# Feed-forward weight loads move from SyncE's DMA queue to GpSimd's in a fused attention and feed-forward block

## The chip, the cores and the metric

The kernel runs on one core of a Trainium2 chip. TensorE (PE) multiplies matrices, VectorE (DVE) and ScalarE (ACT) work element by element, GpSimd (POOL) is a third engine of that kind, and SyncE (SP) issues transfers. The metric is device time in microseconds of one execution; the kernel before took 827.6 us in the median of three runs (826.67, 827.6, 828.36).

## What is computed

One block of a diffusion transformer with adaptive layer norm, 2048 tokens of width 512, 32 heads of 16, and a gated feed-forward part of width 1792:

```
mod = silu(c) @ w_mod                       # six rows: sa, ca, ga, sb, cb, gb
h = layernorm(x) * (1 + ca) + sa
q, k, v = split_heads(h @ wqkv)             # 32 heads of 16
o = softmax(q @ k.T / 4) @ v
x = x + ga * (merge_heads(o) @ wo)
h = layernorm(x) * (1 + cb) + sb
x = x + gb * ((gelu(h @ w_gate) * (h @ w_up)) @ w_down)
```

All inputs and the output are bf16.

## The kernel before

The program is recorded by a planner and then written out. Every operation goes through `rec` (line 190), which finds the semaphores that the operation has to wait for, books it on an engine's list, and hands it to `model` (line 268). `model` keeps the planned free time of each engine and of the DMA engines; the planner places work by these times. The lists are then emitted engine by engine in the order of recording, so each engine, SyncE and GpSimd among them, runs its own list strictly in order. A wait stands ahead of the instruction that needs it and holds up everything behind it on that engine.

The queries are cut into seven sets (`SETS`: 512, 512, 256, 256, 256, 128 and 128 rows). For each set eight groups of four heads are walked, and for each group the keys in blocks. TensorE writes scores into six PSUM banks, three at a time (`qk`). ScalarE takes two or three of the three banks through its exponential into the ring `E`; where it takes two, VectorE takes the third, and makes the exponential from bit operations: one pass out of PSUM per bank (`bits`), and per four banks three passes over 2048 elements in SBUF, `mant`, `square` and `expo` in `power_task`. The products with the values add up in the bank `ps_pv`.

At the end of a group, `unit_end` (line 1554) sends the four softmax sums of each row through memory to have them reciprocated in a better layout: `scr_den<-osb`, `den<-scr_den`, a reciprocal on VectorE, `scr_rec<-rden` and four `rb<-scr_rec`. These are all DMAs on SyncE.

Between the scores, as "side" work, TensorE does the projections and, once a set is finished, its output projection and feed-forward part (`side_ffn`, line 940). For the first four sets (`flow`) the weights are streamed. Gate and up weights come in seven pieces each, of 128 x 4 x 256 elements (256 KB), into a ring of four slots, the columns 0 to 4095 of `mreg`. Four pieces are loaded at the start, and each consumed piece lets the piece four places later be loaded (`load(ci + 4)`, `load(nch + ci + 4)`). The down weights come in seven pieces of 128 x 2 x 512: three at the start into `dreg` (`load_down`), four later into the ring's slots. For the last three sets the whole set of weights is loaded once and kept: `weight_parts` (line 863) makes ten early pieces (`qT` and `xs` as their places), which the main loop issues while the third and fourth sets are worked on, and eleven late ones, issued once the fourth set is done.

All these loads are issued by SyncE, in the same list as the denominators' transfers and the output's. Three lines are enough to see the queue, the ring and the two resident lists:

```
self.dma("sp", ring[i % 4], v[:, :, 2 * P * ci:2 * P * ci + 2 * P], "st%d" % (i % 4))
self.dma("sp", self.wdst[i], v[:, 2 * i:2 * i + 2, :], "sd%d" % i)
return g[:6] + d[:4], u + g[6:] + d[4:]
```

GpSimd only sets some constants at the beginning.

Two more places are touched. `near_end` (line 905) sums the denominators of the last two sets with a matmul on TensorE (`self32`) in place of the way through memory. `fillers` (line 1352) yields matmuls without a use of their result, which keep TensorE busy; one of them writes into the bank `ps_mi`, when no side work has that bank open or when the side work at hand uses the sixth score bank in its place (`fifth`).

Of the kernel before, what the change touches and what calls it, by code (L numbers as in the profile page):

```python
# [14 lines left out]
P = 128  # L15
# [83 lines left out]
class _Recorder:  # L99
# [90 lines left out]
    def rec(self, eng, fn, reads=(), writes=(), dma=None, cost=0.0):  # L190

        if self.dry:
            return None
        stream = eng if dma is None else "d_" + dma
        seq = self.count.get(stream, 0) + 1
        needs = {}

        def need(s, n, raw):
            if s == stream and n == seq:
                return  # L200
            if s == eng == "pe" and dma is None:
                return
            if needs.get(s, 0) < n:
                needs[s] = n

        if dma is not None and seq > 1:
            needs[stream] = seq - 1
        acc = []
        for w, aps in ((False, reads), (True, writes)):
            for ap in aps:  # L210
                r = self._boxes(ap)
                if r is not None:
                    acc.append((w,) + r)
        for w, name, kind, bxs in acc:
            h = self.hist.get(name)
            if not h:
                continue
            for key, ent in h.items():
                for b in bxs:
                    if key[0] < b[1] and b[0] < key[1] and key[2] < b[3] and b[2] < key[3]:  # L220
                        lw, rd = ent
                        if lw is not None:
                            need(lw[0], lw[1], not w)
                        if w:
                            for s, n in rd.items():
                                need(s, n, False)
                        elif kind == "ps":
                            for s, n in rd.items():
                                if s != eng:
                                    need(s, n, False)  # L230
                        break
        at = 0.0
        for s, n in needs.items():
            at = max(at, self.bystream[s][n - 1].t1 + (30 if s == eng else 60))
        if self.probing is not None:
            self.probing = max(self.probing, at)
            self.asked = cost
            return None
        self.count[stream] = seq
        op = _Op(eng, stream, seq, fn)  # L240
        self.bystream.setdefault(stream, []).append(op)
        ck = self.clock[eng]
        for s, n in sorted(needs.items(), key=lambda x: -x[1]):
            if ck.get(s, 0) >= n:
                continue
            prod = self.bystream[s][n - 1]
            prod.inc = True
            op.waits[s] = n
            ck[s] = n
            for k, v in prod.clock.items():  # L250
                if ck.get(k, 0) < v:
                    ck[k] = v
        op.clock = dict(ck)
        for w, name, kind, bxs in acc:
            h = self.hist.setdefault(name, {})
            for b in bxs:
                if w:
                    for key in [k for k in h if b[0] <= k[0] and k[1] <= b[1] and b[2] <= k[2] and k[3] <= b[3]]:
                        del h[key]
                    h[b] = [(stream, seq), {}]  # L260
                else:
                    h.setdefault(b, [None, {}])[1][stream] = seq
        self.ops.append(op)
        self.model(op, max(at, self.free[eng]), cost)
        return op


    def model(self, op, t, cost):
        eng = op.eng
        if op.stream not in COMPUTE:  # L270
            size, run = cost
            self.free[eng] = t + 450
            self.dma_free = max(t + 900, self.dma_free) + size / (320 if run >= 1024 else 245 if run >= 512 else 200)
            op.t1 = self.dma_free + (1000 if run > 64 else 1500)
        elif eng == "pe":
            cols, rows, tp = cost
            mode = 0 if tp is None else (1 if rows == 32 else 2)
            t = max(t, self.pe_issue)
            if mode != self.pe_mode:
                t = max(t, self.pe_end + 105)  # L280
            q = range(16)
            if mode == 1:
                q = range(tp[0] // 8, tp[0] // 8 + 4)
            elif mode == 2:
                q = range(tp[1] // 32, 16, 4)
            t = max(t, max(self.tile_free[i] for i in q))
            end = t + max(cols, 64) / 2.4
            for i in q:
                self.tile_free[i] = end
            self.pe_mode, self.pe_issue, self.pe_end = mode, t + (4 if mode else 27), max(self.pe_end, end)  # L290
            self.free[eng] = t
            self.log.append((t, cols if mode == 0 else cols / 4))
            op.t1 = end + 158
        else:
            self.free[eng] = t + cost
            op.t1 = t + cost + (107 if eng == "act" else 92)
# [151 lines left out]
class _Kernel(_Recorder):  # L448
# [12 lines left out]
    def alloc(self):  # L461
# [32 lines left out]
        self.bufs += [(mreg[:, 4096 + 2048 * i:6144 + 2048 * i], "modB") for i in range(4)]  # L494
        self.bufs.append((wreg[:, 4096:6144], ("q", 3, 3)))
        self.held = set()
        self.two = self.fifth = False
        self.flowing = self.closing = False
        self.wo = sb("wo", [P, 8, D], BF16)
        self.E = sb("E", [P, NSL, 512], BF16)  # L500
# [362 lines left out]
    def weight_parts(self):  # L863

        def part(dst, src, sem):
            return lambda: self.dma("sp", dst, src, sem)
        gv = self.B_w_gate.rearrange("(a p) n -> p a n", p=P)
        uv = self.B_w_up.rearrange("(a p) n -> p a n", p=P)
        dv = self.B_w_down.rearrange("(f p) n -> p f n", p=P)
        g = [part(self.wg[i], gv[:, :, 256 * i:256 * i + 256], "wg%d" % i) for i in range(7)]  # L870
        d = [part(self.wd[i], dv[:, 2 * i:2 * i + 2, :], "wd%d" % i) for i in range(7)]
        u = [part(self.wu[i], uv[:, :, 256 * i:256 * i + 256], "wu%d" % i) for i in range(7)]
        return g[:6] + d[:4], u + g[6:] + d[4:]
# [31 lines left out]
    def near_end(self, k, qd, den):  # L905

        q0, W = SETS[k]
        yield from self.until(("osb", k, qd))
        _, lo, hi = self.osb_span(((k,), qd, q0, W))
        osb, rb = self.osb[:, lo:hi], self.rb[:, lo:hi]  # L910
        yield 4 * W, lambda: self.mm(den, self.self32[:, :], osb)

        def fin():
            self.tt("dve", self.onorm[:, qd, OCOL[k]:OCOL[k] + W], osb, rb, ALU.mult)
        if not self.dry:
            self.task([lambda: self.recip(rb, den)], ("rec", k, qd))
        yield from self.until(("rec", k, qd))
        if not self.dry:
            self.task([fin], ("onorm", k, qd))
        yield END  # L920
# [19 lines left out]
    def side_ffn(self, gi, begin=False):  # L940
# [13 lines left out]
        ring = self.wst[0] + self.wst[1]  # L954
        nch = len(chunks)

        def load(i):
            if flow and i < 2 * nch:
                v = (self.B_w_gate, self.B_w_up)[i // nch].rearrange("(a p) n -> p a n", p=P)
                ci = i % nch  # L960
                self.dma("sp", ring[i % 4], v[:, :, 2 * P * ci:2 * P * ci + 2 * P], "st%d" % (i % 4))
            elif flow:
                load_down(i - 2 * nch + 3)

        def load_down(i):
            if flow:
                v = self.B_w_down.rearrange("(f p) n -> p f n", p=P)
                self.dma("sp", self.wdst[i], v[:, 2 * i:2 * i + 2, :], "sd%d" % i)

        yield from self.until(("ln2", gi))  # L970
        self.flowing = self.flowing or not self.dry
# [200 lines left out]
    def stream(self):  # L1172
# [105 lines left out]
        def acc_of(u):  # L1278
            return self.scp[:, SC - 1, :] if u is units[1] else self.pv[:, :]
# [70 lines left out]
                    cg += 1  # L1350

        def fillers():
            if not self.open or self.fifth:
                yield lambda: self.mm(self.mi[:, :], *filler)
            w = self.next_side()
            if self.open and w is not None:
                self.first = None
                self.probe(w[4][1])
                if self.first is not None and self.first[0].shape[-1] >= P:
                    out, start = self.first  # L1360
                    x = filler[1][:, 0:int(out.shape[-1])]
                    yield lambda: self.mm(out, self.ident[:, :] if start else self.nil[:, :], x, start, start)
            u = next((u for u in units if group[u] == cg and u in begun and left[u]), None)
            if u is not None:
                yield lambda: self.pv_nil(acc_of(u)[:, 0:u[3]], filler[1])

        early, late = self.weight_parts()
        while cg <= group[units[-1]]:
# [7 lines left out]
            t = max(self.pe_now(), virt)  # L1376
# [364 lines left out]
```

## Time and profile before

| | |
|---|---|
| median of three runs | 827.6 us |
| the profiled execution | 826.18 us, span 824.5 us |
| granted TensorE clock | 1.00 |
| ACT busy | 794.4 us |
| DVE busy | 750.9 us |
| PE busy (matmuls) | 750.5 us |
| POOL busy | 4.6 us |
| moved by DMA | 43.73 MB in 76361 packets |
| DMA queue q1 | 76232 packets, 41.82 MB |

The span runs from the first to the last instruction of the profiled execution; the device time of the same execution is 1.7 us longer. Busy time is the sum of an engine's instructions, without waits and without the issuing of DMAs. In a row of instructions, `SPq` and `POOLq` are the sequencers that issue DMAs, `out<-in` are the program's tiles, and "us to landing" is the time from the issue of a DMA until its semaphore has its full count. A line number is often that of a helper (L337 is the matmul in `mm`, L355 the activation, L405 the DMA). TensorE writes 128x512 matmuls as four that use 32 columns of the array each, so one matmul of the source is four in the trace.

### The profile page before, as it was taken

The numbers are of one execution on the slowest core, as the hardware profiler recorded it, in microseconds if no ns is written. First come the engines' busy times: TensorE is split into PE (matmuls) and PEld (weight loads), VectorE is DVE, ScalarE is ACT, GpSimd is POOL, SyncE is SP. The second block draws the span as 40 slices with busy tenths as digits, with TensorE's granted clock in tenths as the row PEclk, the third lists the DMA queues.
The fourth block names the chain that finished last, engine by engine and source line by source line (L and its number), as shares of the span: only waits on it lengthen the run. The fifth ranks groups of instructions, "written<-read, shape, count | busy, mean of one in ns | idle before, by whom it ended". The sixth has DMA issues, their size and how long they took to land.

```text
span 824.5 us, 29810 instructions
## 1 busy us (share of the span) xinstructions
PE 750.5 (91%) x13502; PEld 293.0 (36%) x13502; DVE 750.9 (91%) x1342; ACT 794.4 (96%) x742; POOL 4.6 (1%) x13
## 2 busy tenths in 40 slices
PE   7999998888898998899998989999989989999998
PEld 3333332322222222222333333333443344345556
DVE  7857999999999999999999999999999999889964
ACT  5999999999999999999999999999999999999982
POOL 2000000000000000000000000000000000000000
PEclk9999999999999999999999999999999999999999
DMA  8100000000003211110013212210653243320000
GB/s 286 48 21 18 10 10 8 11 9 10 10 3 97 60 47 35 46 33 20 12 21 98 58 47 58 55 28 12 174 148 109 67 131 97 101 70 11 22 7 14
DMA packets 76361, 43.73 MB, mean 53 GB/s; under 512 B 20557, under 2 KB 74634, under 8 KB 76234
## 3 DMA queue, kind: packets, MB, share of 16 engines
q1 hardware_dynamic: 76232, 41.82, 18.3%
q8 instruction: 106, 1.74, 0.9%
q14 instruction: 21, 0.17, 0.1%
q10 hardware_dynamic: 2, 0.00, 0.0%
HBM read 39.18 MB, written 2.61 MB: 51 GB/s over the span
## 4 chain that ended last, share of the span: by engine, by line
ACT 88%; PE 6%; DVE 3%; DMA 2%; issue 0%; SPq 0%; DVEq 0%
ACT E L355 84%; PE ps_sc L337 3%; ACT hreg L355 3%; PE ps_mi L337 2%; ACT L355 2%; PE ps_pv L337 1%; DMA rb<-scr_rec 1%; DMA scr_rec<-rden 1%; DVE mreg L367 1%; DMA xs<-in_A_x_dram 0%; SPq L405 0%; DVE hreg L376 0%; DVE wreg L367 0%; DVE onorm L359 0%; DVE wreg L359 0%
## 5 line engine op out<-in xcount | busy, mean ns | idle before, releaser
L355 ACT ACTIVATE E<-ps_sc 128x1024 bf16<-128x1024 f32 (+2 forms) x704 | 749.9, 1298 | 14.5 <-PE ps_sc L337 14.2
L337 PE MATMUL ps_sc<-qT,kme 32*128 32x256 bf16 (+2 forms) x1600 | 193.1, 304 | 25.7 <-ACT E L355 21.8
L337 PE MATMUL ps_sc<-qT,kmo 32*128 32x256 bf16 (+2 forms) x1664 | 193.5, 298 | 21.3 <-ACT E L355 18.9
L367 DVE TENSOR_SCALAR mreg<-ps_sc 128x512 uint16<-128x512 f32 x272 | 182.2, 683 | 12.6 <-PE ps_sc L337 10.1
L337 PE MATMUL ps_pv<-E,vaug 128*17 128x256 bf16 (+2 forms) x2540 | 148.9, 300 | 0.9 <-DVE osb L376 0.7
L337 PE MATMUL ps_mi<-wreg,mreg 128*32 128x256 bf16 (+1 forms) x1920 | 110.2, 326 | 8.0 <-ACT hreg L355 2.4
L337 PEld LDWEIGHTS ps_sc<-qT,kme 32*128 32x128 bf16 x1600 | 53.4, 92 | 146.2 <-ACT E L355 124.7
L337 PEld LDWEIGHTS ps_sc<-qT,kmo 32*128 32x128 bf16 x1664 | 54.9, 92 | 132.6 <-ACT E L355 116.4
L367 DVE TENSOR_SCALAR dreg<-ps_sc 128x512 uint16<-128x512 f32 x136 | 91.3, 685 | 7.9 <-PE ps_sc L337 5.9
L337 PEld LDWEIGHTS ps_pv<-E,vaug 128*17 128x17 bf16 x2540 | 51.5, 89 | 53.3 <-issue 39.5
L367 DVE TENSOR_SCALAR mreg<-mreg 128x2048 uint16<-128x2048 uint16 x104 | 70.0, 681 | 0.1
L337 PEld LDWEIGHTS ps_mi<-wreg,mreg 128*32 128x32 bf16 x1920 | 42.4, 95 | 51.0 <-issue 19.6
L337 PE MATMUL ps_pv<-mreg,vaug 128*17 128x256 bf16 (+2 forms) x844 | 49.5, 298 | 3.1 <-DVE mreg L359 2.0
L359 DVE TENSOR_TENSOR mreg<-mreg 128x2048 bf16<-128x2048 bf16 x36 | 43.5, 1207 | 0.1
L337 PE MATMUL ps_mi<-hreg,wreg 128*32 128x512 bf16 x480 | 40.3, 385 | 0.4 <-DVE vaug L376 0.3
L359 DVE TENSOR_TENSOR dreg<-mreg,dreg 128x2048 bf16<-128x2048 bf16 x32 | 38.8, 1216 | 0.1
L359 DVE TENSOR_TENSOR hreg<-ps_mi,hreg 128x512 bf16<-128x512 f32 x48 | 32.8, 684 | 2.9 <-PE ps_mi L337 2.3
L359 DVE TENSOR_TENSOR mreg<-dreg,mreg 128x2048 bf16<-128x2048 bf16 x28 | 34.0, 1213 | 0.0
L337 PE MATMUL ps_mi<-wo,onorm 128*32 128x512 bf16 x416 | 32.1, 383 | 0.4 <-DVE qT L367 0.2
L376 DVE CAST hreg<-ps_mi 128x512 bf16<-128x512 f32 x46 | 31.4, 683 | 1.1 <-PE ps_mi L337 0.8
L337 PE MATMUL ps_mi<-xs,ident 128*32 128x512 bf16 (+1 forms) x376 | 30.7, 380 | 0.8 <-DVE hreg L359 0.8
L337 PE MATMUL ps_mi<-mreg,hreg 128*32 128x512 bf16 x384 | 31.1, 385 | 0.0
(161 smaller groups left out, 673.7 us busy)
## 6 DMA issues: line engine op xcount, KB each, us to landing
mreg<-in_B_w_up_dram SPq DMA_DIRECT2D x32, 256.0 KB, 3.0
mreg<-in_B_w_gate_dram SPq DMA_DIRECT2D x28, 256.0 KB, 3.5
mreg<-in_B_w_down_dram SPq DMA_DIRECT2D x16, 256.0 KB, 2.8
dreg<-in_B_w_down_dram SPq DMA_DIRECT2D x12, 256.0 KB, 4.6
mreg<-in_w_mod_dram SPq DMA_DIRECT2D x1, 2048.0 KB, 12.1
rb<-scr_rec SPq DMA_DIRECT2D x64, 32.0 KB, 1.8
out_dram<-xs SPq DMA_DIRECT2D x16, 128.0 KB, 1.7
rb<-scr_rec SPq DMA_DIRECT2D x116, 16.0 KB, 2.1
```

Of the source, the lines that this page charges most:

```text
L337: return self.rec("pe", lambda e: e.matmul(out, lhsT, rhs, start=start, stop=stop, tile_position=tp), [lhsT, rhs, *after], [out], cost=(n, ...
L355: return self.rec("act", lambda e: e.activation(out, in_, func, scale=scale, **kw), rd, wr, cost=self.cost("act", out, [in_], "act") + load)
L359: return self.rec(eng, lambda e: e.tensor_tensor(out, a, b, op), [a, b], [out], cost=self.cost(eng, out, [a, b], "tt"))
L367: return self.rec(eng, lambda e: e.tensor_scalar(out, a, s1, s2, **kw), rd, [out], cost=self.cost(eng, out, [a], "ts") + (60 if len(rd) > ...
L376: return self.rec(eng, lambda e: e.tensor_copy(out, in_), [in_], [out], cost=self.cost(eng, out, [in_], "ts"))
```

## The change

All loads of `w_gate`, `w_up` and `w_down`, streamed and resident, are issued by GpSimd. The planner goes on charging them to SyncE's planned time (`self.free["sp"]`), so that it places the rest as it did. A flag `sums` holds back the filler into `ps_mi` while a denominator sum lies there. The instructions on TensorE, VectorE and ScalarE, their order and their waits are the same in both programs; SyncE's list is shorter by 105 DMAs, GpSimd's is longer by as many. The loads keep their order among themselves.

```diff
@@ rec
-        self.model(op, max(at, self.free[eng]), cost)
+        self.model(op, max(at, self.free[eng if dma is None else "sp"]), cost)
@@ model
-            self.free[eng] = t + 450
+            self.free["sp"] = t + 450
@@ alloc
-        self.two = self.fifth = False
+        self.two = self.fifth = self.sums = False
@@ weight_parts
         def part(dst, src, sem):
-            return lambda: self.dma("sp", dst, src, sem)
+            return lambda: self.dma("pool", dst, src, sem)
@@ near_end
+        self.sums = True
         yield 4 * W, lambda: self.mm(den, self.self32[:, :], osb)
...
         yield from self.until(("rec", k, qd))
+        self.sums = False
@@ side_ffn
-                self.dma("sp", ring[i % 4], v[:, :, 2 * P * ci:2 * P * ci + 2 * P], "st%d" % (i % 4))
+                self.dma("pool", ring[i % 4], v[:, :, 2 * P * ci:2 * P * ci + 2 * P], "st%d" % (i % 4))
...
-                self.dma("sp", self.wdst[i], v[:, 2 * i:2 * i + 2, :], "sd%d" % i)
+                self.dma("pool", self.wdst[i], v[:, 2 * i:2 * i + 2, :], "sd%d" % i)
@@ fillers
-            if not self.open or self.fifth:
+            if not self.open or self.fifth and not self.sums:
```

GpSimd's list runs in order too. A load there waits for the matmuls that last read its place, and for nothing that stood between the loads in SyncE's list. The semaphores are unchanged.

## The prediction

> **What bounds the kernel now.** I read the busy totals first, then the chain that ended last, then the stretches in which feed-forward weights are loaded.
>
> ```profile
> span 824.5 us, 29810 instructions
> PE 750.5 (91%) x13502; PEld 293.0 (36%) x13502; DVE 750.9 (91%) x1342; ACT 794.4 (96%) x742; POOL 4.6 (1%) x13
> ACT 88%; PE 6%; DVE 3%; DMA 2%; issue 0%; SPq 0%; DVEq 0%
> 249.00:793.00 544.00, 500.49 (x9598) 197.75 (x9590) 513.61 (x885) 542.35 (x497) 0.00 (x0) 1.00 0.23 63
> 249.00:375.00 126.00, 113.72 (x1402) 31.86 (x1394) 122.43 (x194) 125.95 (x115) 0.00 (x0) 1.00 0.19 52
> 443.00:529.00 86.00, 78.63 (x1469) 29.08 (x1464) 81.00 (x139) 84.94 (x74) 0.00 (x0) 1.00 0.27 72
> 576.00:635.00 59.00, 53.24 (x1240) 26.14 (x1240) 55.19 (x94) 58.54 (x55) 0.00 (x0) 1.00 0.52 146
> 653.00:704.00 51.00, 46.20 (x1082) 22.18 (x1076) 49.43 (x88) 50.95 (x49) 0.00 (x0) 1.00 0.43 117
> ```
>
> The windows list, after length, the busy time of PE, weight loads, DVE, ACT and POOL. ScalarE's exponentials set the end. The first weights go out at 249.49 us (row below) and the last exponential ends near 793; there ScalarE is busy 542.35 of 544.00 us. So in the whole stretch that the change can touch, 1.65 us of ScalarE idle time is to be had, and no more. VectorE stands close behind: in the four loading windows its idle time is 3.57, 5.00, 3.81 and 1.57 us, 13.95 together.
>
> These are the places where ScalarE's feeding did break, from the chain in order of time:
>
> ```profile
> 474.01 0.07 SPq L405
> ...
> 475.81 3.35 DMA rb<-scr_rec
> ...
> 582.02 5.53 DMA scr_rec<-rden
> SPq L405 <- PE ps_mi L337: 56.8, 27, 5.9
> SPq L405 <- PE ps_sc L337: 46.8, 23, 7.1
> ```
>
> SyncE's queue is in order. It stands 103.6 us in total waiting for matmuls to release a weight buffer, and a softmax denominator's four small transfers queue behind such a wait: at 474 the chain passes through SyncE and then 3.35 us of a reciprocal's way back, at 582 through 5.53 us of its way out. That is what the change can mend.
>
> **The change, part by part.**
>
> *Two edits that only steer the planner* (SyncE's planned free time is charged for the loads as before; a filler is held back while a denominator sum lies in the shared bank): the two programs have the same instructions with the same waits on TensorE, VectorE and ScalarE. Cost nothing, with nothing to hide.
>
> *105 loads leave SyncE for GpSimd* (7 gate, 7 up and 7 down pieces for each of four streamed stages and for the resident set). Gain: SyncE's waits for TensorE go, so the denominators come earlier. ScalarE's idle time above bounds it at 1.65 us; below, at nothing, since VectorE may not be ready earlier either. The chain legs at 474 and 582 are part of it, not all: I take 0.7.
>
> *Earlier starts.* GpSimd's queue holds nothing else, so a stage's first seven loads go when the stage before has read its last down piece:
>
> ```profile
> 249.49 2.08 SPq L405 DMA_DIRECT2D mreg<-in_B_w_gate_dram  x4
> 410.32 0.40 PE L337 MATMUL ps_mi<-mreg,hreg 128*32 128x512 bf16 x4
> 443.50 2.09 SPq L405 DMA_DIRECT2D mreg<-in_B_w_gate_dram  x4
> 449.66 0.83 PE L337 MATMUL ps_mi<-wreg,mreg 128*32 128x512 bf16 x12
> 576.60 3.17 SPq L405 DMA_DIRECT2D mreg<-in_B_w_gate_dram  x4
> 580.91 0.84 PE L337 MATMUL ps_mi<-wreg,mreg 128*32 128x256 bf16 x24
> 582.45 2.59 SPq L405 DMA_DIRECT2D mreg<-in_B_w_gate_dram  x2
> 590.94 0.62 PE L337 MATMUL ps_mi<-wreg,mreg 128*32 128x256 bf16 x16 [0.35 <-DVE hreg L376]
> 619.12 0.42 SPq L405 DMA_DIRECT2D mreg<-in_B_w_down_dram  x1
> 624.77 0.61 PE L337 MATMUL ps_mi<-mreg,hreg 128*32 128x512 bf16 x8
> ```
>
> About 411 instead of 443.5 in the second stage. The shortest leads of a first piece, 449.66 - 443.50 = 6.2 and 580.91 - 576.60 = 4.3 us, grow, the first by some 33 us. Gain: none, since those matmuls didn't wait.
>
> *Loads in the middle of a stage* go as before, when the matmuls of four pieces back release their slot. The fifth piece of the third stage is issued at 582.45 and used at 590.94, 8.5 us later; the last down piece goes at 619.12 and is used at 624.77, 5.65 us later. The landing times of that window:
>
> ```profile
> mreg<-in_B_w_gate_dram SPq DMA_DIRECT2D x7, 256.0 KB, 4.2
> mreg<-in_B_w_down_dram SPq DMA_DIRECT2D x4, 256.0 KB, 3.0
> ```
>
> So 4.3 us (8.5 - 4.2) and 2.65 us (5.65 - 3.0) may be added before a matmul waits. If that cover goes, TensorE stands, the next scores are late, and ScalarE idles one for one.
>
> *What a load costs on GpSimd.* No row of before shows it, as GpSimd is done after 59 us. A gate or up piece is 128 x 4 runs of 512 bytes, 512 reads and 512 writes to be listed; a down piece is half as many of 1024 bytes. The nearest rows:
>
> ```profile
> 0.80 0.20 POOL L383 MEMSET nil<- 128x128 bf16 x1 [0.29 <-POOLq L1726]
> 2.17 2.26 POOL L383 MEMSET vaug<- 128x512 bf16 x1
> 4.03 1.25 POOL L383 MEMSET rb<- 128x1024 f32 x1
> 58.76 0.31 POOL L386 TENSOR_SCALAR_AFFINE_SELECT self<-self 128x128 f32<-128x128 f32 x1 [53.47 <-DVE self L383]
> L405 SPq DMA_DIRECT2D mreg<-in_B_w_up_dram x7: 368/378/505, 590.8 to 608.9; - x7
> ```
>
> Lower end: as quick as SyncE, 0.37 us. Upper end: 1,024 entries at the rate of the slow memset (2.26 us for 512), 4.5 us. I take the memset of 1,024 elements as nearest, one element an entry: 1.25 us for gate and up, and by the line through both quick memsets (0.20 + 384 x 1.05/896) 0.65 us for down. At that price the third stage's queue is 20 x 1.25 + 11 x 0.65 = 32 us of work in 59, and 1.25 us stays inside the 4.3 and 2.65 us of cover: no late matmul. At 4.5 us it would be some 115 us of work in 59.
>
> *What it costs VectorE.* VectorE is the next engine to become late. Two kinds of its passes stand out:
>
> ```profile
> L367 DVE TENSOR_SCALAR mreg<-ps_sc 128x512 uint16<-128x512 f32 x272 | 182.2, 683 | 12.6 <-PE ps_sc L337 10.1
> L367 DVE TENSOR_SCALAR mreg<-mreg 128x2048 uint16<-128x2048 uint16 x104 | 70.0, 681 | 0.1
> L367 DVE TENSOR_SCALAR dreg<-dreg 128x2048 uint16<-128x2048 uint16 x40 | 27.2, 679 | 0.0
> L367 DVE TENSOR_SCALAR dreg<-mreg 128x2048 uint16<-128x2048 uint16 x32 | 21.6, 683 | 0.0
> L367 DVE TENSOR_SCALAR mreg<-dreg 128x2048 uint16<-128x2048 uint16 x28 | 18.9, 679 | 0.0
> PEld ps_sc L337 <- DVE mreg L367: 3.6, 8, 0.9
> 714.27 2.13 SPq L405 DMA_DIRECT2D mreg<-in_B_w_up_dram  x4
> 704.00:793.00 89.00, 83.97 (x2132) 43.08 (x2124) 76.85 (x141) 88.95 (x86) 0.00 (x0) 1.00 0.18 47
> ```
>
> From SBUF to SBUF it does 2,048 elements in 0.68 us, from PSUM 512 in the same time. The wide passes (204, 0.25 per us of the span) use a path four times as wide; if GpSimd needs part of that path while it writes its lists, such a pass waits. A pass that wants to start while a load of length T is being written waits T/2 on average, so a load costs 0.25 x T x T/2: 0.195 us at 1.25, 0.053 at 0.65. Stages one, two and four: 14 x 0.195 + 7 x 0.053 = 3.1 us each; the third, with ten resident pieces among its own, 20 x 0.195 + 11 x 0.053 = 4.5. Lower end nothing (no shared path), upper end as T grows, by its square. The cover is VectorE's idle time of the window, of which I let two thirds help, because a delay has to meet idle time before a matmul needs the bank (the wait row: score matmuls already wait for VectorE's passes). What is left: 3.1 - 2.4 = 0.7; 3.1 - 3.3, nothing; 4.5 - 2.5 = 2.0; 3.1 - 1.05 = 2.05: 4.7 us. The last eleven loads, at 714, meet a stretch in which VectorE has 12 us to spare: nothing.
>
> The Trainium skill, page "SBUF — State Buffer", section "Who interferes with whom", says that VectorE and GpSimd share one pair of SBUF ports as an exclusive lock, taken by VectorE's two-port passes, and that a DMA issued from GpSimd needs it to write descriptors. The same page gives about 620 ns for such a DMA alone; as an estimate from that figure, 94 loads at 0.25 x 0.62 x 0.62/2 make 4.5 us, inside the cover, and the sum would be no change. No run here shows either yet.
>
> *Sum.* 826.2 (the profiled execution; span 824.5) + 4.7 - 0.7 = 830.2. The median of the runs shown, 827.6, is 1.4 above the profiled execution; I forecast 831.6 for a median.
>
> **The rivals.**
>
> *No change* (chance 0.27, 827.6 within 1.7): a load takes GpSimd well under 1 us, or the wide passes share nothing with it. For it: at T = 0.65 for all, 94 x 0.053 = 5 us fall inside VectorE's 13.95. Against: VectorE's idle time is 2 to 6% and in pieces.
>
> *Faster* (0.07): the freed SyncE queue is all that matters, and the denominators' way through memory no longer stands behind loads. Place: the chain legs at 474 and 582. Price: all 1.65 us of ScalarE's idle time, 825.9; it decides once VectorE loses less than some 1 us in all. Against: it has to recover every gap, and 31.5 us after 793 don't contain a load.
>
> The Trainium skill, page "DMA: Bandwidth & Descriptors", section "Issuing engines are not separate DMA queues", holds that another issuer saves only the sequencer's issue time. By that there is no gain either; the trace's bound agrees.
>
> *GpSimd too slow for the ring* (0.16): at T of 2 us or more the third stage's queue nears 40 + 11 us of 59 while the passes lose 62 x 0.5 + 32 x 0.125 = 35 us, 26 beyond the cover: 853; with 4.5 us per piece TensorE waits for weights too, 115 - 59 = 56 us in the third stage alone, 880 and over. Against: the nearest row is 1.25.
>
> *My forecast*, some microseconds lost through VectorE: 0.50, between 829.3 and 848 (at T = 1.8: 62 x 0.405 + 32 x 0.10 = 28.3, less 9.3 of cover, + 19).
>
> **How the numbers follow.** 0.2%, 1.7 us, is about what a measurement of this kernel tells from no change. Faster 0.07, same 0.27, slower 0.50 + 0.16 = 0.66. The likeliest gives 831.6. The range goes from 826.0 (the bound on the gain) to 848 (the forecast's end at T = 1.8); it leaves out half of the faster case and nearly all of the third rival, some 0.18. The forecast's own range is 829.3 to 848.
>
> **What would show it.** Right: wide passes of more than 0.68 us mean or gaps ahead of them, mostly between 249 and 704; more ScalarE idle time than 1.65 us there, released by score matmuls that waited for VectorE; the second stage's loads at about 411; SyncE's waits for TensorE gone. Wrong: passes unchanged with ScalarE idle as before (no change); matmuls on weights that wait for a DMA (the ring), and landing times of 6 us and more; or ScalarE's idle time below 0.5 us (faster). If VectorE's rows are unchanged and the time is longer all the same, the mechanism is wrong whatever the total.

## The result and the profile after

| | before | after |
|---|---|---|
| median | 827.6 us (826.67 to 830.12, 5 runs) | 837.07 us (835.56 to 838.9, 5 runs) |
| ratio | 1 | 1.0115, 95% interval 1.0099 to 1.0131 |
| span of the profiled execution | 824.5 us | 835.3 us |

The change costs 9.5 us between the medians, and the two profiled spans lie 10.8 us apart. From the page after: busy totals, GpSimd's DMA queue (packets, MB, share) and the shares of the chain that ended last.

```profile
PE 755.4 (90%) x13502; PEld 293.7 (35%) x13502; DVE 752.7 (90%) x1342; ACT 796.2 (95%) x742; POOL 84.4 (10%) x118
q0 software_dynamic: 8400, 27.53, 11.4%
ACT 72%; PE 13%; DVE 7%; DMA 7%; SPq 1%; issue 1%; DVEq 0%
```

The busy times of VectorE and ScalarE hardly moved (+1.8 us each), so the time went into waits. In the chain, ScalarE gave up 16 points; PE, DMA and VectorE took them. The windows after say where (columns as in the prediction: start and end, length, busy PE, weight loads, DVE, ACT, POOL, then the granted clock, the DMA share and GB/s; 576 to 635 and 704 to 793 are left out, the sum has them):

```profile
249.00:375.00 126.00, 114.02 (x1402) 31.73 (x1398) 122.66 (x194) 125.95 (x115) 10.34 (x14) 1.00 0.15 37
375.00:443.00 68.00, 60.33 (x971) 19.75 (x968) 61.67 (x100) 63.06 (x60) 5.44 (x7) 0.95 0.15 42
443.00:529.00 86.00, 78.68 (x1483) 29.38 (x1482) 82.55 (x146) 85.95 (x75) 10.35 (x14) 1.00 0.19 48
529.00:576.00 47.00, 44.25 (x860) 16.72 (x859) 43.33 (x80) 45.76 (x42) 5.16 (x7) 1.00 0.23 65
635.00:653.00 18.00, 15.51 (x288) 6.04 (x280) 14.84 (x28) 15.44 (x14) 5.15 (x7) 0.91 0.43 117
653.00:704.00 51.00, 45.95 (x1042) 21.38 (x1040) 47.52 (x88) 49.42 (x45) 9.68 (x12) 0.97 0.25 66
sum 544.00, PE 496.30 PEld 193.03 DVE 507.94 ACT 532.96 POOL 74.28; mean PE 62.04 PEld 24.13 DVE 63.49 ACT 66.62 POOL 9.29
```

ScalarE's idle time between 249 and 793 is 544.00 - 532.96 = 11.04 us, against 1.65 before: 9.4 us more. The spans differ by 10.8, and the rest is about the 1.8 us by which ScalarE's busy time grew. The idle time isn't spread over the stages in which GpSimd writes lists. Nearly all of it lies in 375 to 443 (4.94), 529 to 576 (1.24), 635 to 653 (2.56) and 653 to 704 (1.58). In the first three of these the kernel before had no idle time at all; its rows for the first and the third:

```profile
375.00:443.00 68.00, 63.01 (x1049) 21.18 (x1053) 66.45 (x114) 68.00 (x64) 0.00 (x0) 1.00 0.07 17
635.00:653.00 18.00, 16.39 (x350) 6.66 (x346) 17.14 (x37) 18.00 (x17) 0.00 (x0) 1.00 0.12 24
```

The window in which SyncE's wait had cost something, 443 to 529, did get better: 1.06 us of idle time became 0.05. The granted clock fell to 0.95, 0.91 and 0.97 in three of the windows in which TensorE stood; before, it was 1.00 there. What the lower clock adds to the loss no run separates.

Now the timeline after around 409 to 427: start, duration, engine, line, operation, and in brackets the idle time of the engine before it and its releaser.

```profile
408.86 0.75 POOL L405 DMA_DIRECT2D mreg<-in_B_w_gate_dram  x1 [45.66 <-PE ps_mi L337]
410.69 2.59 POOL L405 DMA_DIRECT2D mreg<-in_B_w_gate_dram  x3 [1.08 <-PE ps_mi L337]
412.10 0.25 DVE L379 RECIPROCAL rden<-den 128x16 f32<-128x16 f32 x1
412.37 0.32 SPq L405 DMA_DIRECT2D scr_rec<-rden  x1
413.26 2.12 POOL L405 DMA_DIRECT2D dreg<-in_B_w_down_dram  x3
417.99 2.73 SPq L405 DMA_DIRECT2D rb<-scr_rec  x4
422.22 0.69 DVE L359 TENSOR_TENSOR onorm<-osb,rb 128x512 bf16<-128x512 f32 x1 [3.44 <-DMA rb<-scr_rec]
422.97 0.62 PE L337 MATMUL ps_mi<-wo,onorm 128*32 128x512 bf16 x4 [3.56 <-DVE onorm L359]
424.17 2.10 ACT L355 ACTIVATE E<-ps_sc 128x1024 bf16<-128x1024 f32 x2 [3.71 <-PE ps_sc L337]
427.20 1.45 ACT L355 ACTIVATE E<-ps_sc 128x1536 bf16<-128x1536 f32 x1 [0.93 <-PE ps_sc L337]
```

The same place before:

```profile
412.44 0.24 DVE L379 RECIPROCAL rden<-den 128x16 f32<-128x16 f32 x1
412.71 1.38 SPq L405 DMA_DIRECT2D scr_rec<-rden  x1
415.19 1.71 SPq L405 DMA_DIRECT2D rb<-scr_rec  x4
419.05 0.68 DVE L359 TENSOR_TENSOR onorm<-osb,rb 128x512 bf16<-128x512 f32 x1
419.78 0.10 PEld L337 LDWEIGHTS ps_mi<-wo,onorm 128*32 128x32 bf16 x4 [0.31 <-DVE onorm L359]
```

Follow the denominator. The reciprocal is ready at the same time in both (412.10 and 412.44), and its way out is issued at the same time too (412.37 and 412.71). But the way back starts 2.5 us after that issue before and 5.6 us after it now, since seven weight loads of 256 KB (1.8 MB) went out between 408.86 and 415.4. The transfers of 404 to 428, median landing in the last column, after and then before:

```profile
rb<-scr_rec SPq DMA_DIRECT2D x4, 32.0 KB, 2.9
scr_rec<-rden SPq DMA_DIRECT2D x1, 8.0 KB, 5.6
```

```profile
rb<-scr_rec SPq DMA_DIRECT2D x4, 32.0 KB, 1.9
scr_rec<-rden SPq DMA_DIRECT2D x1, 8.0 KB, 2.5
```

So 3.1 us on the way out and 1.0 on the way back. The DMA engines were busy meanwhile; the windows 413 to 420, after and then before, with the DMA share and GB/s last:

```profile
413.00:420.00 7.00, 5.99 (x120) 2.18 (x113) 5.75 (x9) 7.00 (x8) 2.38 (x4) 1.00 0.81 244
413.00:420.00 7.00, 6.55 (x130) 2.41 (x128) 6.86 (x12) 7.00 (x8) 0.00 (x0) 1.00 0.19 33
```

That the small transfers are late because they share these engines is read from such shares and from the landing times; no run shows it packet by packet. Both consumers stand in order. VectorE's list has the normalization `onorm` next, and the passes that take the next scores out of PSUM lie behind it. TensorE's list has the output projection of `onorm`, with scores behind it. This denominator had little time to spare: before, its last `rb` transfer landed at 418.32 and `onorm` began at 419.05, 0.7 us later, and TensorE's weight load waited 0.31 us for `onorm`. A delay of 4.1 us less 0.7 is the wait of 3.44 us, and it reaches ScalarE as 3.71 + 0.93 us. Two later stalls are of the same kind, one step of a denominator each:

```profile
565.21 0.43 DVE L359 TENSOR_TENSOR onorm<-osb,rb 128x256 bf16<-128x256 f32 x1 [1.85 <-DMA rb<-scr_rec]
566.72 5.52 ACT L355 ACTIVATE E<-ps_sc 128x1536 bf16<-128x1536 f32 x4 [1.23 <-PE ps_sc L337]
647.42 0.20 DVE L379 RECIPROCAL rden<-den 128x8 f32<-128x8 f32 x1 [2.88 <-DMA den<-scr_den]
649.17 1.02 ACT L355 ACTIVATE E<-ps_sc 128x1024 bf16<-128x1024 f32 x1 [2.13 <-PE ps_sc L337]
```

Each stands behind an early group of seven loads, at 555.37 and at 636.71. If the exponentials of the two traces are matched one by one, after falls behind before by 5.0 us at 421 and 422, 1.4 at 561, 3.8 from 641 to 646 and 0.8 at 670, and catches up by 1.3 at 481 and 0.5 at 594 (positions in before's time). The first stall is the largest, but not the whole loss. The theory after this reading: **the first seven loads of a stage lost an order that nobody had written down**. In SyncE's list they stood behind the transfers of the running denominators; on GpSimd they start earlier and share the DMA engines with those. That alone isn't enough for a stall: the first stage's loads start 49 us early, beside a denominator as well, and cost nothing. That denominator had 3.0 us to spare: before, its last `rb` landed at 205.83, for an `onorm` at 208.80. After, it lands at 208.47, and the normalization follows with hardly a wait:

```profile
200.96 0.34 SPq L405 DMA_DIRECT2D scr_rec<-rden  x1
203.60 1.49 POOL L405 DMA_DIRECT2D mreg<-in_B_w_gate_dram  x2 [2.01 <-PE ps_pv L337]
203.80 1.71 SPq L405 DMA_DIRECT2D rb<-scr_rec  x4
208.60 0.69 DVE L359 TENSOR_TENSOR onorm<-osb,rb 128x512 bf16<-128x512 f32 x1
```

### The profile page after: what moved, and what is told of

The parts are those of the page before. It is cut to its first block, busy times and chain, and to the rows that moved or that the text cites. A ratio compares the mean times of both kernels' runs of the same rounds, so it can differ in the third digit from the quotient of the medians.

```text
span 835.3 us, 29812 instructions
## 1 busy us (share of the span) xinstructions
PE 755.4 (90%) x13502; PEld 293.7 (35%) x13502; DVE 752.7 (90%) x1342; ACT 796.2 (95%) x742; POOL 84.4 (10%) x118
## 3 DMA queue, kind: packets, MB, share of 16 engines
q0 software_dynamic: 8400, 27.53, 11.4%
## 4 chain that ended last, share of the span: by engine, by line
ACT 72%; PE 13%; DVE 7%; DMA 7%; SPq 1%; issue 1%; DVEq 0%
ACT E L355 68%; PE ps_sc L337 5%; PE ps_mi L337 5%; ACT hreg L355 2%; PE ps_pv L337 2%; DMA den<-scr_den 2%; DMA scr_rec<-rden 2%; DMA rb<-scr_rec 2%; DVE mreg L367 2%; DMA scr_den<-osb 1%; ACT L355 1%; DVE dreg L367 1%; SPq L405 1%; DVE hreg L359 1%; DVE wreg L359 0%
## 5 line engine op out<-in xcount | busy, mean ns | idle before, releaser
L405 POOL DMA_DIRECT2D mreg<-in_B_w_gate_dram x28 | 21.6, 772 | 410.3 <-PE ps_mi L337 231.9
L405 POOL DMA_DIRECT2D mreg<-in_B_w_up_dram x32 | 25.1, 784 | 127.0 <-PE ps_mi L337 122.6
L359 DVE TENSOR_TENSOR onorm<-osb,rb 128x256 bf16<-128x256 f32 (+2 forms) x51 | 24.7, 486 | 8.6 <-DMA rb<-scr_rec 8.4
```

Of the source, the lines that this page charges most:

```text
L359: return self.rec(eng, lambda e: e.tensor_tensor(out, a, b, op), [a, b], [out], cost=self.cost(eng, out, [a, b], "tt"))
L405: return e.dma_start(out, in_)
```

## Experiments

Ratios are to the kernel before, timed on the same chip. Unless said otherwise the planned order on TensorE, VectorE and ScalarE is that of both kernels. The "gate" used below is an extra wait: `dma` and `rec` get an argument `after`, and the wait goes ahead of the load. `rstd` is a tile that VectorE writes shortly before the stage begins.

**E1, the early start undone, GpSimd kept.**

```diff
-                self.dma("pool", ring[i % 4], ..., "st%d" % (i % 4))
+                self.dma("pool", ring[i % 4], ..., "st%d" % (i % 4),
+                         after=[self.rstd[:, tiles[0]:tiles[0] + 1]] if i == 0 else ())
```

> All 105 loads stay on GpSimd, but the first load of each streamed stage waits for the set's reciprocal standard deviation on VectorE, so that a stage's first seven loads go out at about 444, 576 and 654 us, as before the change, in place of 409, 555 and 637. Theory burst (the seven early loads run into a denominator's transfers that TensorE and VectorE then wait for): 826 to 829 us, ScalarE idle at most 2 us between 249 and 793. Theory queue (whatever GpSimd's queue carries, its large packets hold up SyncE's small transfers): 832 or more. Theory VectorE (the forecast: wide passes wait while GpSimd writes its lists): 835 to 838, as 105 lists are still written.

Measured: 827.99 us, ratio 1.0002 (0.999 to 1.0014). GpSimd issues all 105 loads, and nothing is lost, as the burst theory expected. The loads of the second stage now go at 447 and the window 375 to 443 has no idle time. So GpSimd's lists and its queue cost nothing on balance that this interval would show (0.14%, 1.2 us); the early start does.

**E2 and E3, the loads divided.** E2 has the first seven of each stage on GpSimd, early, and the other 77 on SyncE. E3 has it the other way round for the streamed stages: the first seven of each on SyncE, at their old place, the later ones and ten resident pieces on GpSimd, the last eleven on SyncE. The pieces of a ring slot that go through different queues use semaphores of their own.

```diff
-                self.dma("pool", ring[i % 4], ...)
+                self.dma("pool" if i < 4 else "sp", ring[i % 4], ...)
-                self.dma("pool", self.wdst[i], ...)
+                self.dma("pool" if i < 3 else "sp", self.wdst[i], ...)
```

These lines are E2's; in E3 the two engines change places.

> Only the first seven loads of each streamed stage go through GpSimd (28 of 105, early as in the changed kernel); the other 77 go through SyncE as before. Theory burst: 834 to 838 us, nearly the whole loss. Theory queue: at most a third of the loss, about 830. Theory VectorE: 28/105 of the lists, about 830.

> The other way round: the first seven loads of each stage and the eleven late resident ones go through SyncE, in SyncE's old order; the 66 loads in the middle of the stages go through GpSimd. Theory burst: 826 to 829 us. Theory queue: 831 to 835, since small transfers and GpSimd's loads are mixed for most of the time. Theory VectorE: 66/105 of the loss, about 833.

Measured: E2 836.92 us, ratio 1.012 (1.0104 to 1.0137); E3 827.61, ratio 1.0002 (0.9989 to 1.0015). Both lie where the burst theory put them: the 28 early loads make the whole loss, within the noise. E2's wide VectorE passes are as before (the largest group, by line and shape: count, total us, mean ns):

```profile
L367 DVE TENSOR_SCALAR mreg<-mreg 128x2048 uint16<-128x2048 uint16 x104 | 70.3, 683 | 0.1
```

The time is 9 us longer with VectorE's rows unchanged, which the prediction had named as the sign that its mechanism is wrong.

**E4, the early start without GpSimd.** All loads are on SyncE; the first seven of stages two to four are recorded right behind the previous stage's last output, where GpSimd's queue would start them. The planner charges them at the old place.

```diff
+        if gi + 1 < FLOW and not self.dry:
+            self.ahead = []
+            for i in range(4):
+                load(i)
+            for i in range(3):
+                load_down(i)
+            self.early, self.ahead = self.ahead, None
```

> No load on GpSimd. The kernel before, but the first seven loads of stages two to four stand in SyncE's list right behind the last output of the stage before, at about 412, 555 and 634 us. The other engines' lists are unchanged. Theory burst: 833 to 838 us, the loss without GpSimd. Theory queue and theory VectorE: 827 to 828, no loss, as every load is SyncE's.

Measured: 848.56 us, ratio 1.0259 (1.0245 to 1.0274). That is twice the loss and above the 833 to 838 that I expected. The timeline at the same denominator:

```profile
414.18 3.17 SPq L411 DMA_DIRECT2D mreg<-in_B_w_gate_dram  x4
414.29 0.25 DVE L385 RECIPROCAL rden<-den 128x16 f32<-128x16 f32 x1
417.39 1.53 SPq L411 DMA_DIRECT2D dreg<-in_B_w_down_dram  x3
418.96 0.47 SPq L411 DMA_DIRECT2D scr_rec<-rden  x1
```

Here the reciprocal's way out also waits for SyncE to issue seven loads, 4.4 us from 414.54 to 418.96, and then takes 5.3 us to land. I had left this second delay out. Without GpSimd the loss is there all the same; with the second queue, where the small transfer at least is issued on time, it is half as large.

**E5 and E7, fewer loads in flight.** E5 lets each of the first seven loads wait until the one before has landed. E7 starts only the four gate pieces early and gates the three down pieces as in E1.

```diff
@@ E5, gate pieces, then down pieces
+ after=[ring[i - 1]] if 0 < i < 4 else ()
+ after=[ring[3] if i == 0 else self.wdst[i - 1]] if i < 3 else ()
@@ E7, down pieces
+ after=[self.rstd[:, tiles[0]:tiles[0] + 1]] if i == 0 else ()
```

> As the changed kernel, with the early bursts at the same places, but within a stage's first seven loads each waits until the one before has landed, so one early load is in flight at a time. Theory backlog (a small transfer is late because it shares the DMA engines with several queued loads): 827 to 830 us. Theory early bytes (early loads hurt by when they run, however many are queued): 834 to 838.

> Four loads of each burst early, the three down loads held back to the old time. Theory backlog: a part of the loss that goes with the load count, 4/7 of 9 us at most, 830 to 834 us. Theory early bytes: the same fraction. If the loss is all or nothing (any late reciprocal stalls VectorE for a whole step): 836 to 838.

Measured: E5 833.0 us, ratio 1.0061 (1.0037 to 1.0085), between both expectations; E7 835.97, ratio 1.0092 (1.0072 to 1.0113), above the 830 to 834 of a loss that goes with the number of loads and just under the 836 to 838 of one that is all or nothing. The way out of the denominator at 413, and the wait in front of its normalization in E5:

```profile
scr_rec<-rden SPq DMA_DIRECT2D x1, 8.0 KB, 3.8
422.10 0.69 DVE L364 TENSOR_TENSOR onorm<-osb,rb 128x512 bf16<-128x512 f32 x1 [2.66 <-DMA rb<-scr_rec]
```

```profile
scr_rec<-rden SPq DMA_DIRECT2D x1, 8.0 KB, 5.2
```

The first fence is E5, the second E7. One load in flight already makes 3.8 us out of 2.5 (2.0 to 2.7 in before, E1, E8 and E9, where no early load is there), four make 5.2, seven 5.6. Matched with before, the exponentials of E5 and E7 both fall behind by 3.8 us at 421 and 422, those of after by 5.0. So for this stall one load is as bad as four. What parts E5 from E7 lies later: E7 loses 3.0 us from 561 to 564 and E5 hardly anything there. Why the paced loads spare that place was not followed further.

**E6, a new plan.** The planner itself places and charges the early loads, on GpSimd, and so orders all engines anew.

```diff
-        self.model(op, max(at, self.free[eng if dma is None else "sp"]), cost)
+        self.model(op, max(at, self.free[eng]), cost)
+        if gi + 1 < FLOW and not self.dry:
+            for i in range(4):
+                load(i)
+            for i in range(3):
+                load_down(i)
```

> GpSimd's early bursts stay, seven loads at once, but the planner records them where they run, behind the stage before, and charges them to GpSimd's own planned time; it then orders TensorE, VectorE and ScalarE anew. Theory plan (the loss comes from VectorE's list, laid out for transfers that are not disturbed at that place): 825 to 831, the loss mostly gone, with a microsecond or two of luck in the new order. Theory share (a burst beside a denominator's transfers costs wherever it stands): 833 to 838.

Measured: 839.91 us, ratio 1.0152 (1.0133 to 1.0172), above both expectations. The first stall is gone, but there are others:

```profile
375.00:443.00 68.00, 63.18 (x1080) 21.88 (x1072) 66.70 (x109) 68.00 (x66) 5.45 (x7) 1.00 0.17 44
DVE onorm L359 <- DMA rb<-scr_rec: 10.1, 9, 2.2
```

Read the first line against after's row of this window (63.06 us of ScalarE, here all 68.00), the second (wait: total us, times, longest) against 3.9 us in before and 8.4 in after. This run mixes the new order with other work: ScalarE is busy 800.1 us, 5.7 more than before, and there are 13586 matmuls for 13502. It doesn't tell whether a plan can use the early loads.

**E8, E9 and E10, one stage, three places.** Stages one, three and four are gated as in E1. The second stage's loads go as in after (E10), wait for the last `rb` transfer of the denominator that stalled (E8), or for that of the next one (E9).

```diff
@@ E10
+ after=[self.rstd[...]] if i == 0 and gi != 1 else ()
@@ E8
+ after=() if i else [self.rbs[-3]] if gi == 1 else [self.rstd[...]]
```

`rbs` lists the last `rb` transfer of each denominator recorded so far; E9 has `self.rbs[-2]`.

> Only the second stage's first loads start early (about 409 to 411), all other stages are gated as in E1. If the stages' losses add up, this one has its own 5.0 us at 421 to 422 and nothing else: 832 to 834, with the onorm wait of about 3.4 us on rb and ScalarE idle 4 to 5 us between 409 and 443. If a delay of the early stage is soaked up by the later ones (the kernel waits there in any case), 828 to 830.

> The seven first loads of the second stage wait for the last transfer of the denominator under way at 409 to 418 (its fourth rb<-scr_rec), so they go at about 418; the other stages are gated as in E1. Collision theory (what counts is which small transfers the loads meet, and whether the normalization behind these is due): the first denominator is clear, onorm near 419 to 422 has no wait, but the loads then meet the next denominator's scr_rec (422) and rb (424): a later wait of 2 to 4 us, 829 to 832. Rival (it is the early start itself, whatever the loads meet: loads ahead of the plan always take about 5 us): 832 to 834. Second rival (only this one denominator is short of time): 827 to 829.

> As the run before, but the loads wait for the next denominator's last rb transfer, so they go at about 426, still 17 us ahead of the old place. They meet only the following denominator's first two transfers (428 to 432 in the kernel before), whose reciprocal is not issued on until 435.7, so that there is room. Collision theory: no wait at onorm, no idle time of ScalarE at 421, 827 to 829. Rival (early start itself): 831 to 834, with ScalarE idle between 426 and 443.

| loads at | run | median, us | ratio (95%) | wait ahead of the first `onorm` | ScalarE idle, 405 to 443 |
|---|---|---|---|---|---|
| 412 to 419 | E10 | 834.72 | 1.0084 (1.0061 to 1.0108) | 3.61 us | 4.58 us |
| 418 to 424 | E8 | 828.95 | 1.002 (1.0008 to 1.0032) | none | 0.00 us |
| 430 to 435 | E9 | 830.09 | 1.0025 (1.0006 to 1.0043) | none | 0.00 us |
| 447 (E1) | E1 | 827.99 | 1.0002 (0.999 to 1.0014) | none | 0.00 us |

The window 405 to 443 and the normalization in E10, then in E8, with E8's start of the loads:

```profile
405.00:443.00 38.00, 32.28 (x606) 11.99 (x606) 32.81 (x54) 33.42 (x31) 5.44 (x7) 0.96 0.23 60
425.71 0.69 DVE L364 TENSOR_TENSOR onorm<-osb,rb 128x512 bf16<-128x512 f32 x1 [3.61 <-DMA rb<-scr_rec]
```

```profile
405.00:443.00 38.00, 35.47 (x694) 13.56 (x694) 36.75 (x66) 38.00 (x35) 5.07 (x7) 1.00 0.23 63
418.45 2.96 POOL L415 DMA_DIRECT2D mreg<-in_B_w_gate_dram  x4 [54.90 <-PE ps_sc L347]
419.05 0.69 DVE L369 TENSOR_TENSOR onorm<-osb,rb 128x512 bf16<-128x512 f32 x1
scr_rec<-rden SPq DMA_DIRECT2D x1, 4.0 KB, 4.0
```

Six microseconds later, still 25 ahead of the old place, the same loads cost 1.5 us in the median (E8) and 2.7 (E9, between its two expectations), against 7.3 in E10. Both intervals just exclude no loss, and where these small rests come from is open: ScalarE has no idle time between 405 and 443 in either. That falls against "any early start costs", and partly against my own expectation too: E8's loads do delay the next denominator's way out (4.0 us; 1.4 in before), but no normalization waits for it.

The time to spare says why. Before, E8's denominator landed at 428.23 for an `onorm` at 434.02: 5.8 us to spare, of which E8 uses 1.8. The one that E9's loads meet had only 0.13 us (442.33 and 442.46), but it is hardly later: its `onorm` waits 0.31 us, and ScalarE doesn't notice. So a stall needs two things at once: loads in flight, and a delay larger than the denominator has to spare. In this stage only the one at 412 meets both.

E10's median lies 6.7 us above E1's, more than the 4.58 us of idle time in its window. The two profiled executions, 834.37 and 829.42, differ by 4.95, nearly all of it at this stall, and E10's shows no second one; so the rest is likely the spread of four runs.

## Why the prediction was wrong

It had the sign, and 837.07 lies inside its range, but that is luck: the microseconds came from a place that it had priced at nothing. Several of its signs of being right came true as well (ScalarE idle for more than 1.65 us, the early loads, SyncE's waits for TensorE gone). They come out alike under both mechanisms, and only the wide passes tell the two apart.

*What bounds the kernel*: held. ScalarE's idle time between 249 and 793 is 9.4 of the 10.8 us between the profiled spans.

*The edits that steer the planner*: at nothing, and E1, which has both and times as before, agrees.

*105 loads leave SyncE*, 0.7 us taken, 1.65 as the bound: SyncE's 103.6 us of waits for TensorE are gone, and the exponentials catch up 1.3 us at 481 in after, E1 and E3 alike, and 0.5 more at 594 in after and E1. The step at 594 is in E2 and E4 too, whose loads are on SyncE there, so it isn't owed to the queue alone. In E1 and E3 later steps of 0.4 to 2.1 us take the gain back, and neither beats the kernel before.

***Earlier starts*: the step that failed.** The time was right, "about 411" (408.86), and so was "Gain: none, since those matmuls didn't wait". But I asked only who gains from an early load and not what the loads meet on the DMA engines. Denominator transfers were costed in the SyncE step as what gets free, and not here as what is in the way. E1 and E2 put the whole loss on this step, and E10 against E8 shows the place: a denominator with 0.7 us to spare, made 4.1 us late. The later stalls were not tested one by one.

The rows to look at were in the trace of before: the last `rb` landing at 418.32 for an `onorm` at 419.05, and the output projection's weight load at 419.78 with its wait of 0.31 us for `onorm`. Of a landing that grows from 2.5 to 5.6 us, 0.7 us has cover there.

*Loads in the middle of a stage*: held; E3 leaves them on GpSimd and loses nothing in the median.

*What a load costs on GpSimd*, 1.25 us for gate and up, 0.65 for down: both came out near 0.75. The rows list count, busy time and mean ns:

```profile
L405 POOL DMA_DIRECT2D mreg<-in_B_w_up_dram x32 | 25.1, 784 | 127.0 <-PE ps_mi L337 122.6 <-PE ps_sc L337 4.4
L405 POOL DMA_DIRECT2D mreg<-in_B_w_down_dram x16 | 11.4, 710 | 55.0 <-PE ps_mi L337 50.3 <-PE ps_pv L337 4.7
```

Half as many runs in a down piece take 9% less time, so the entries that I counted are not what a list costs; the third rival, a ring too slow, never came near.

*What it costs VectorE*, 4.7 us: a real effect, mis-sized and covered. The four groups of wide passes take 139.8 us together after, against 137.7:

```profile
L367 DVE TENSOR_SCALAR mreg<-mreg 128x2048 uint16<-128x2048 uint16 x104 | 71.3, 693 | 0.1
```

Matched by time, 28 of the 204 passes overlap a list and average 743 ns; the others, 682. Of the 28, 25 began while the list was already being written; they average 750, and the longest took 892. The premise that a pass waits for the rest of the list (T/2, some 0.37 us) is off by a factor of six, and by E1 the 2 us which are left find cover. The Trainium skill, page "SBUF — State Buffer", section "Who interferes with whom", says that whoever comes second at the shared ports is fully blocked for the whole instruction; with 0.06 us for each overlap, the trace here disagrees in size.

*The sum*, 830.2, was 4.0 above its profiled execution for the wrong reason. The range's end of 848 isn't what its own terms give, either: 826.2 + 19 - 0.7 + 1.4 is 845.9. The rival "no change" is what the same loads do once they are gated (E1).

The second page that the prediction drew on, "DMA: Bandwidth & Descriptors", section "Issuing engines are not separate DMA queues", says that transfers of different issuers interleave on the same 16 engines. The landing of 5.6 us agrees with that. It also says that another issuer only saves issue time. Here that is not all: it also took away an order, at 9.5 us.

## What to carry to other kernels

An in-order queue is also a schedule: before moving transfers to a queue of their own, list what stood ahead of them, compute when they would start without it, and look for small transfers in flight at that time. For each, read from the old trace the time between its last landing and the start of its consumer. If that is less than the delay to be feared, replace the lost order by an explicit wait, as E1 and E8 do. And a mended version that equals the old one (E1) says that the queue was never the bound.

## What the runs showed of the hardware

- A list for a 256 KB load took GpSimd 0.71 to 0.78 us in the two groups above, nearly the same for 512 runs of 512 bytes as for 256 of 1024.
- The software queue moved 27.53 MB in 8400 packets, 80 for each load and 3.3 KB each; SyncE's queue had 76232 packets for 41.82 MB before, some 550 bytes each. No run here shows a gain from the larger packets: the gate pieces land in 3.6 us in the median after and in 3.5 before, the up pieces in 3.4 and in 3.0.
- The early start of the same loads on SyncE (E4) cost twice what it did on GpSimd: in one queue the small transfer was issued 4.4 us late, behind the loads, and then still took 5.3 us to land.
- Between profiled executions the exponentials can already be shifted by up to 2.5 us at 12 us after the start (E10 against before), long before any weight is loaded. A difference of that size between two single profiles says nothing about a change.
